# Block 0's taps split between two engines, and an order written out by hand that runs one block further

## The chip, the cores and the metric

The kernel runs on one core of a Trainium2 chip. The metric is device time in microseconds, the median of three runs: 1071.19 us before the change (1070.69 to 1071.75). The engines are named as in the profile: PE (TensorE, the matrix products), DVE (VectorE), ACT (ScalarE), POOL (GpSimd), and SP (SyncE), whose queue starts the transfers here.

## The reference

A causal attention of seven taps comes first. For every token and each of 8 heads a softmax over 7 numbers weights the token's own row and the 6 rows before it; a head is 24 of the 192 channels. Its output, 16384 tokens by 192 channels, goes through a feed-forward layer of 2048 columns with the gate `h * sigmoid(1.702 h)`:

```python
w = softmax(weight_gen, axis=-1)                      # (4, 4096, 8, 7)
x_unf = x_pad[:, idx, :].reshape(B, S, K, H, group)   # 7 rows for each token
x = np.einsum('bshk,bskhg->bshg', w, x_unf)           # (4, 4096, 192)
h = x.reshape(16384, 192) @ w_in                      # (16384, 2048)
g = h / (1 + exp(-1.702 * h))
out = g @ w_out                                       # (16384, 192)
```

The weights arrive as 64-bit floats and the output is 32-bit. The precision wanted is that of 32-bit products; most of the kernel reaches it with several 16-bit ones.

## The kernel before

**Tiling.** The 16384 tokens are cut into 32 blocks of 512, and the 2048 hidden columns into 16 slices of 128. One block times one slice is a unit, numbered 0 to 511. For a unit, PE fills one PSUM bank with h (128 columns by 512 tokens). In the program's order list `W.n` is the part of h that comes from channels 0 to 127 (line 446 to 449 from block 1 on, line 442 in block 0), and `X.n` does the part from channels 128 to 191 for the four units 4n to 4n+3 together. `gt` and `gm` are the gate (a tanh on ACT, line 469, and a product on DVE, line 474); `gh` and `gl` split the gated value into two 16-bit halves (ACT line 479, DVE line 481), after which the bank is free; `S.n` multiplies it by the output weights (line 495 to 497).

**Attention.** `a2.3` is step 3 of block 2: POOL multiplies 768 numbers in each partition by a tap's weights (line 190), and `a2.3p` adds them to the sum (line 206). The softmax steps are `s2.0` to `s2.6`: a maximum on DVE (line 154), a subtraction on POOL (line 156), an exponential on ACT, a sum and a reciprocal on DVE (lines 160 and 168), a product on POOL (line 174).

**Between the two.** `c2.0` finds block 2's largest value for its scale (DVE line 273, then one small PE product called `top`, line 255). `x2.0` to `x2.2` split the block into 16-bit parts (ACT line 312, DVE line 315), and `tu2` and `xd2` start the transposing transfers `xt` and a copy of part of it, `xd` (lines 321 and 325) on SP's queue.

**Block 0** is different: it is not split, and PE works on its 32-bit numbers. Its taps are multiplied one by one, five on DVE and two on POOL (`dtap`, `ptap`), two pairs are summed on DVE (`sum`), and PE turns and adds what is left (`tr.n`, line 231). `keep` copies the result to SBUF (lines 303 and 306). Meanwhile ACT and DVE narrow the weights: `nm`, `nb`, `n1`, `n2` from 64 to 32 bits (lines 374 to 394), and `na`, `bin`, `bout`, `ph`, `pl`, `ps` to 16-bit halves, of which `pl` is DVE's (line 421). `hold.A`, `hold.B` and `hold.C` let POOL copy 8 numbers out of a weight tile (line 615), so that POOL goes on only when DVE has finished that tile.

**What sets the order.** Every engine works through its own instructions in program order. Up to unit 31 (blocks 0 and 1) that order is the list ORDER, in which units take turns in four banks (`few = 2 * NF`, lines 433 to 435). From block 2 on a planner emits units by sixes in six banks, and each side step (scales, split, softmax, attention) has a due place in units. Since no place lies before `few`, the first planned block's scale is asked for right at that border (line 649).

## Time and profile before

| | |
|---|---|
| median of three runs | 1071.19 us |
| the profiled execution, as timed | 1072.55 us |
| its span, first to last instruction | 1070.3 us |
| busy in the span | PE 99%, DVE 80%, POOL 68%, ACT 64% |
| granted TensorE clock, mean | 0.995 |

PE is nearly always busy, so the time of this kernel is PE's work plus whatever PE waits for. All of what it waits for lies in the first 120 us: the slices of the page show PE busy to nine tenths or more from there to the last slice but one. The profiled execution is 2.25 us longer than its span and 1.36 us longer than the median.

### The profile page before, as it was taken

How to read it: one execution, taken by the hardware profiler on the slowest of the kernel's cores; microseconds unless marked ns; L12 is line 12 of the kernel's file. 1: busy time of each engine (PE TensorE's matmuls, PEld its weight loads, DVE VectorE, ACT ScalarE, POOL GpSimd, SP SyncE). 2: the span in 40 equal slices, each digit the busy share in tenths (PEclk: the TensorE clock that was granted, in tenths of full speed). 3: DMA queues.
4: the chain of work that ended last, by engine and by line, in shares of the span. 5: the costliest groups of instructions: out<-in, count | busy, mean ns of one | idle time of the engine just before them, and what ended most of it. 6: DMA issues, size and time to landing. Idle time of an engine off the chain costs nothing.

```text
span 1070.3 us, 22014 instructions
## 1 busy us (share of the span) xinstructions
...
## 2 busy tenths in 40 slices
...
GB/s 312 105 52 18 93 31 79 33 18 94 33 91 19 69 43 33 93 25 39 79 18 93 33 93 17 33 78 33 94 33 86 23 33 79 33 31 36 16 34 15
DMA packets 73454, 60.70 MB, mean 57 GB/s; under 512 B 60556, under 2 KB 66188, under 8 KB 71816
## 3 DMA queue, kind: packets, MB, share of 16 engines
...
q14 instruction: 34, 0.28, 0.1%
q10 hardware_dynamic: 288, 0.20, 0.1%
...
## 4 chain that ended last, share of the span: by engine, by line
PE 90%; DVE 4%; ACT 3%; POOL 2%; issue 1%; POOLq 0%; ACTq 0%
PE o L495 16%; PE o L497 15%; PE o L496 15%; PE h L446 10%; PE h L447 10%; PE h L449 10%; PE h L448 10%; PE h L463 5%; PE tr L231 1%; POOL acc L206 1%; POOL prod L190 1%; ACT g L479 1%; DVE g L474 1%; DVE h L474 0%; ACT wos L382 0%
## 5 line engine op out<-in xcount | busy, mean ns | idle before, releaser
L495 PE MATMUL o<-wos,g 128*128 128x192 f16 x1984 | 489.4, 247 | 0.0
L497 PE MATMUL o<-woh,g 128*128 128x192 f16 x1984 | 488.6, 246 | 0.0
L496 PE MATMUL o<-wol,g 128*128 128x192 f16 x1984 | 488.6, 246 | 0.0
L474 DVE SCALAR_TENSOR_TENSOR h<-th,h 128x512 f32<-128x512 f32 x496 | 335.9, 693 | 167.4 <-ACT th L469 159.3
L469 ACT ACTIVATE th<-h,s 128x512 f32<-128x512 f32 x496 | 332.5, 688 | 212.9 <-PE h L464 126.2
L206 POOL TENSOR_TENSOR acc<-acc,prod 128x768 f32<-128x768 f32 x186 | 344.6, 1852 | 14.4
L481 DVE SCALAR_TENSOR_TENSOR g<-g,h 128x512 f16<-128x512 f16 x496 | 338.3, 683 | 12.9 <-ACT g L479 1.2
L479 ACT ACTIVATE g<-h 128x512 f16<-128x512 f32 x496 | 296.5, 598 | 51.0 <-DVE h L474 51.0
L190 POOL TENSOR_TENSOR prod<-xb,wb 128x768 f32<-128x768 f32 x186 | 291.9, 1569 | 10.9
L495 PEld LDWEIGHTS <-g 128*128 128x128 f16 x1984 | 194.2, 98 | 73.8 <-issue 34.9
L496 PEld LDWEIGHTS <-g 128*128 128x128 f16 x1984 | 194.3, 98 | 35.6 <-issue 0.7
L497 PEld LDWEIGHTS <-g 128*128 128x128 f16 x1984 | 194.3, 98 | 0.0
L446 PE MATMUL h<-xt,w0l 128*128 128x512 f16 x496 | 188.7, 380 | 1.6 <-DVE s L261 1.3
L449 PE MATMUL h<-xt,wth 128*128 128x512 f16 x496 | 188.7, 381 | 0.0
L448 PE MATMUL h<-xt,w0h 128*128 128x512 f16 x496 | 188.7, 381 | 0.0
L447 PE MATMUL h<-xt,w0h 128*128 128x512 f16 x496 | 188.7, 381 | 0.0
L174 POOL TENSOR_TENSOR wb<-wb,wr 128x224 f32<-128x224 f32 x31 | 17.8, 575 | 209.0 <-DVE wr L168 198.0
L315 DVE SCALAR_TENSOR_TENSOR xs<-acc,s,xs 128x512 f16<-128x512 f32 (+1 forms) x62 | 91.7, 1518 | 0.3 <-ACT xs L312 0.3
L448 PEld LDWEIGHTS <-w0h 128*128 128x128 f16 x496 | 48.7, 98 | 59.0 <-issue 0.8
L449 PEld LDWEIGHTS <-wth 128*128 128x128 f16 x496 | 48.7, 98 | 59.0 <-issue 0.8
L463 PE MATMUL h<-xt,tl 64*128 64x512 f16 x248 | 67.9, 380 | 0.0
L464 PE MATMUL h<-xd,tl 64*128 64x512 f16 x248 | 67.9, 380 | 0.0
...
## 6 DMA issues: line engine op xcount, KB each, us to landing
...
```

The lines of the kernel that those rows point to most:

```text
L190: eng.tensor_tensor(to.rearrange("p j (h g) -> p (j h) g", g=G), xv, wv, ALU.mult)
L206: nc.gpsimd.tensor_tensor(acc, acc, t, ALU.add)
L446: nc.tensor.matmul(ps, lhsT=w0l[:, s], rhs=x0, start=start, stop=False)
L448: nc.tensor.matmul(ps, lhsT=w0h[:, s], rhs=x0, start=False, stop=False)
L449: nc.tensor.matmul(ps, lhsT=th_[:, s], rhs=x1, start=False, stop=stop)
L469: nc.scalar.activation(t, hp[u], AF.Tanh, scale=scale[u[0]][:, 4:5] if u[0] else SIG / 2)
L474: nc.vector.scalar_tensor_tensor(to, th.pop(u), 1.0, hp[u], ALU.add, ALU.mult)
L479: nc.scalar.activation(g[:, 0], hp[u], AF.Copy, scale=2.0**-12)
L481: nc.vector.scalar_tensor_tensor(g[:, 1], g[:, 0], -(2.0**12), hp.pop(u), ALU.mult, ALU.add)
L495: nc.tensor.matmul(o, lhsT=lo, rhs=wos[:, d], start=a and j % 2 == 0, stop=False, skip_group_check=True)
L496: nc.tensor.matmul(o, lhsT=hi, rhs=wol[:, d], start=False, stop=False, skip_group_check=True)
L497: nc.tensor.matmul(o, lhsT=hi, rhs=woh[:, d], start=False, stop=z, skip_group_check=True)
```

## The change

The attention of block 0 is divided by channels. DVE multiplies all seven taps for the first 6 heads (144 channels), and PE turns and adds channels 0 to 127 of them in one bank (`ta`, `tr`). POOL multiplies the last three heads (72 channels) and sums the taps in three groups for channels 128 to 191 (`tb`, with `p` for the sums); PE turns these three sums in another bank, two groups of 64 columns at a time (`trb`). `ka` and `kb` copy the results out in halves and quarters. Block 0's own softmax is subtracted on DVE instead of POOL.

ORDER now covers units 0 to 47, three blocks (`few = 3 * NF`), and the planner starts with block 3. The holds are no longer in the list. The first input weights are loaded ahead of the tail of channels.

On POOL, at the start of the program, this stood before (`tap` is block 0's, `acc` and `prod` are block 1's attention):

```order
L156 TENSOR_TENSOR wb<-wb,wm 128x224 x2
L184 TENSOR_TENSOR x_107<-wb,wr 128x224
L190 TENSOR_TENSOR tap<-xb,x_107 128x768 x2
L174 TENSOR_TENSOR wb<-wb,wr 128x224
L190 TENSOR_TENSOR acc<-xb,wb 128x768
```

and this stands there now:

```order
L193 TENSOR_TENSOR x_107<-wb,wr 128x224
L165 TENSOR_TENSOR wb<-wb,wm 128x224
L234 TENSOR_TENSOR rest<-xb,x_107 128x288 x2
L269 TENSOR_TENSOR rests<-rest 128x256
L234 TENSOR_TENSOR rest<-xb,x_107 128x288 x2
L269 TENSOR_TENSOR rests<-rest 128x256
L234 TENSOR_TENSOR rest<-xb,x_107 128x288 x2
L269 TENSOR_TENSOR rests<-rest 128x256
L234 TENSOR_TENSOR rest<-xb,x_107 128x288
L269 TENSOR_TENSOR rests<-rests,rest 128x256
L183 TENSOR_TENSOR wb<-wb,wr 128x224
L199 TENSOR_TENSOR acc<-xb,wb 128x768
```

Two long products became seven short ones and four sums, ahead of block 1's attention.

Further on POOL, in block 2's attention, where the first two holds stood:

```order
L206 TENSOR_TENSOR acc<-acc,prod 128x768
L156 TENSOR_TENSOR wb<-wb,wm 128x224
L615 COPY held<-w0l 128x8
L190 TENSOR_TENSOR prod<-xb,wb 128x768
L206 TENSOR_TENSOR acc<-acc,prod 128x768
L190 TENSOR_TENSOR prod<-xb,wb 128x768
L206 TENSOR_TENSOR acc<-acc,prod 128x768
L615 COPY held<-wol 128x8
```

and now, from block 2's second product on:

```order
L199 TENSOR_TENSOR prod<-xb,wb 128x768
L165 TENSOR_TENSOR wb<-wb,wm 128x224
L215 TENSOR_TENSOR acc<-acc,prod 128x768
L199 TENSOR_TENSOR prod<-xb,wb 128x768
L215 TENSOR_TENSOR acc<-acc,prod 128x768
L183 TENSOR_TENSOR wb<-wb,wr 128x224
L199 TENSOR_TENSOR prod<-xb,wb 128x768
L215 TENSOR_TENSOR acc<-acc,prod 128x768
```

No copy waits for a weight tile any more. The product with `wr` (line 183, step `s3.6` of block 3's softmax) now stands between block 2's third and fourth tap, and it needs a reciprocal from DVE. That reciprocal stands here on DVE, at the end of block 0 (`xs` is block 1's split, `w0l`, `tl` and `wol` are narrowed weights, `g` block 0's gates):

```order
L374 SCALAR_TENSOR_TENSOR xs<-acc,s,xs 128x4x128
L374 SCALAR_TENSOR_TENSOR xs<-acc,s,xs 128x4x64
L480 SCALAR_TENSOR_TENSOR w0l<-ri,sc,w0h 128x1024
L480 SCALAR_TENSOR_TENSOR tl<-rt,sc,th 128x1024
L533 SCALAR_TENSOR_TENSOR g_576<-th,h 128x512
L533 SCALAR_TENSOR_TENSOR g_583<-th,h 128x512
L480 SCALAR_TENSOR_TENSOR wol<-ro,sc,woh 128x1024 x2
L533 SCALAR_TENSOR_TENSOR g_605<-th,h 128x512
L480 SCALAR_TENSOR_TENSOR w0l<-ri,sc,w0h 128x1024
L177 RECIPROCAL wr<-wm 128x32
```

Before, the same stretch of DVE read:

```order
L315 SCALAR_TENSOR_TENSOR xs<-acc,s,xs 128x4x128
L315 SCALAR_TENSOR_TENSOR xs<-acc,s,xs 128x4x64
L260 TENSOR_REDUCE tm<-top 128x1
L261 TENSOR_SCALAR sums<-tm 128x1
L265 TENSOR_SCALAR sc<-sums 128x1
L266 TENSOR_SCALAR sc<-sc 128x1
L267 TENSOR_SCALAR sc<-sc 128x1
L283 TENSOR_SCALAR s<-s,sc 128x1
L474 SCALAR_TENSOR_TENSOR g_549<-th,h 128x512
L421 SCALAR_TENSOR_TENSOR tl<-rt,sc,th 128x1024
```

The scale for the input weights (`sc`) used to be worked out after block 1's split, and the output weights' scale and `wol` only in block 1; both scales now come ahead of the split, and two of the three `wol` pieces and both of `w0l` ahead of that reciprocal.

The diff, of the table its first and last lines only:

```diff
--- before.py
+++ after.py
@@ -20,27 +20,36 @@
 ONE = float(1 << 23)
 
 ORDER = """
-warm.11 s1.0 s0.0 s1.1 s0.1 s0.2 s0.3 s0.4 s0.5 s0.6 s0.7 ptap.1 dtap.5 dtap.2 tr.5 ptap.3 dtap.6 dtap.4
...
+s0.0 warm.8 s0.1 s0.2 s0.3 s0.4 s0.5 s1.0 s0.7 s0.6 s1.1 s1.2 ta.5 tb.0 tb.1 ta.6 tr.5 nm.i0 tb.1p ta.0 tr.6
...
+gt.47 a4.5p gm.47 gm.46 a4.6 gh.46 gh.47 gl.46 gl.47 a4.6p
 """
 TURNED = [a for a in ORDER.split() if a.startswith("tr.")]
+OTHERS = ((0, 1), (2, 3), (4, 5, 6))
 
 
 @with_exitstack
@@ -206,32 +215,72 @@
                 nc.gpsimd.tensor_tensor(acc, acc, t, ALU.add)
             yield
 
-    turned, taps, added = [], {}, []
-
-    def first_tap(k, by):
+    HA = -(-P // G)
+    turned, taps, added, rest = {}, {}, [], {}
+
+    def first_tap(k, eng):
+
         if k < K - 2:
-            t = apool.tile([P, J, D], F32, tag="tap", name="tap", bufs=K - 2)
+            taps[k] = apool.tile([P, J, HA * G], F32, tag="tap", name="tap", bufs=K - 2)
         else:
-            t = opool.tile([P, J, D], F32, tag="osb", name="tap")
-        taps[k] = t
-        tap(0, {"dve": nc.vector, "pool": nc.gpsimd}[by], t, k, near[by])
+            taps[k] = opool.tile([P, J, D], F32, tag="osb", name="tap")[:, :, 0 : HA * G]
+        near_tap(eng, taps[k], k, 0, HA)
+
+    def near_tap(eng, to, k, h0, h1):
+        n = h1 - h0
+        w = near["dve" if eng is V else "pool"].rearrange("p (j h) k -> p j h k", h=H)[:, :, h0:h1, k]
+        for j0 in range(0, J, 4):
+            xv = xb[0][:, j0 + k : j0 + k + J, h0 * G : h1 * G].rearrange("p j (h g) -> p j h g", g=G)
+            eng.tensor_tensor(
+                to.rearrange("p j (h g) -> p j h g", g=G), xv,
+                w.unsqueeze(3).to_broadcast([P, J, n, G]), ALU.mult,
+            )
 
     def add_taps(k, l):
-        nc.vector.tensor_tensor(taps[k], taps[k], taps[l], ALU.add)
+        nc.vector.tensor_tensor(taps[k][:, :, 0:P], taps[k][:, :, 0:P], taps[l][:, :, 0:P], ALU.add)
 
     def turn_tap(k):
 
 
-        if not turned:
-            turned.extend(ps_h.tile([P, N], F32, tag=f"h{i}", name="tr") for i in (1, 2))
+        if "a" not in turned:
+            turned["a"] = ps_h.tile([P, N], F32, tag="h1", name="tr")
         start, stop = not added, len(added) == len(TURNED) - 1
         added.append(k)
-        for ps, c, n in zip(turned, (0, P), (P, C1)):
-            for j in range(J):
-                nc.tensor.matmul(
-                    ps[:n, j * P : (j + 1) * P], lhsT=taps[k][:, j, c : c + n], rhs=ident,
-                    start=start and j == 0, stop=stop, skip_group_check=True,
-                )
+        for j in range(J):
+            nc.tensor.matmul(
+                turned["a"][:, j * P : (j + 1) * P], lhsT=taps[k][:, j, 0:P], rhs=ident,
+                start=start and j == 0, stop=stop, skip_group_check=True,
+            )
+
+    def rest_tap(k):
+
+        if not rest:
+            rest["sums"] = apool.tile([P, J, D], F32, tag="acc", name="rests").rearrange("p j d -> p (j d)")
+            rest["taps"] = apool.tile([P, J, D], F32, tag="prod", name="rest", bufs=1).rearrange("p j d -> p (j d)")
+        n = len(rest)
+        n = n % 2 * J * (D - (H - 3) * G)
+        t = rest[k] = rest["taps"][:, n : n + J * 3 * G].rearrange("p (j c) -> p j c", j=J)
+        near_tap(G_, t, k, H - 3, H)
+
+    def rest_sum(k):
+        g, at = next((g, i * J * C1) for i, g in enumerate(OTHERS) if k in g)
+        to = rest["sums"][:, at : at + J * C1].rearrange("p (j c) -> p j c", j=J)
+        a, b = (rest[l][:, :, 3 * G - C1 : 3 * G] for l in (g[0], k))
+        nc.gpsimd.tensor_tensor(to, a if k == g[1] else to, b, ALU.add)
+
+    def turn_rest(k):
+
+
+        if "b" not in turned:
+            turned["b"] = ps_h.tile([P, N], F32, tag="h2", name="tr")
+        i = [g[0] for g in OTHERS].index(k)
+        at, start, stop = i * J * C1, not rest.get("turned"), i == len(OTHERS) - 1
+        rest["turned"] = True
+        for q in range(J // 2):
+            nc.tensor.matmul(
+                turned["b"][:, q * P : (q + 1) * P], lhsT=rest["sums"][:, at + 2 * q * C1 : at + 2 * (q + 1) * C1], rhs=ident,
+                start=start and q == 0, stop=stop, skip_group_check=True,
+            )
 
     scale = {}
     inv_w, unit = sc[:, 0:1], sc[:, 1:2]
@@ -296,14 +345,24 @@
 
     x32 = [const.tile([P, N], F32, name=f"x32{c}") for c in range(2)]
 
-    def keep(n):
-
-
-        if n == 2:
-            nc.vector.tensor_copy(x32[1][C1:P], turned[1][0:C1])
+    def keep_a(n):
+
+        h = slice(n * N // 2, (n + 1) * N // 2)
+        if n:
+            nc.vector.tensor_copy(x32[0][:, h], turned["a"][:, h])
         else:
-            p = (P, C1)[n]
-            nc.scalar.copy(x32[n][0:p], turned[n][0:p])
+            nc.scalar.copy(x32[0][:, h], turned["a"][:, h])
+
+    def keep_b(n):
+
+
+        r, h = n % 2, n // 2
+        to = x32[1][h * C1 : (h + 1) * C1].rearrange("p (q r t) -> p q r t", r=2, t=P)[:, :, r]
+        of = turned["b"][r * C1 : (r + 1) * C1, 0 : N // 2].rearrange("p (q t) -> p q t", t=P)
+        if r == h:
+            nc.scalar.copy(to, of)
+        else:
+            nc.vector.tensor_copy(to, of)
 
     def split_x(blk):
         xs[blk] = t = tpool.tile([P, J, 2 * D], F16, tag="xs", name="xs", bufs=2)
@@ -517,7 +576,7 @@
 
 
     units = [(blk, f) for blk in range(NB) for f in range(NF)]
-    few = 2 * NF
+    few = 3 * NF
 
     def first(n):
 
@@ -551,8 +610,8 @@
     with tc.manual_schedule():
         load_w(0)
         load_x(0, 0, J)
+        load_in(0)
         load_tail(0)
-        load_in(0)
         load_in(1)
         load_x(0, J, XB * J)
         load_in(2)
@@ -578,15 +637,19 @@
             if a in ("s0.6", "s0.7"):
                 weights_near(("dve", "pool")[a == "s0.7"])
             elif k[0] == "s" and k[1:].isdigit():
-                step(k, softmax, int(k[1:]))
-            elif k in ("dtap", "ptap"):
-                first_tap(int(n), {"d": "dve", "p": "pool"}[k[0]])
+                step(k, softmax, int(k[1:]), G_ if int(k[1:]) else V)
+            elif k in ("ta", "pta"):
+                first_tap(int(n), V if k == "ta" else G_)
+            elif k == "tb":
+                (rest_sum if n[-1] == "p" else rest_tap)(int(n.rstrip("p")))
+            elif k == "trb":
+                turn_rest(int(n))
             elif k == "sum":
                 add_taps(*map(int, n.split(".")))
             elif k == "tr":
                 turn_tap(int(n))
-            elif k == "keep":
-                keep(int(n))
+            elif k in ("ka", "kb"):
+                (keep_a if k == "ka" else keep_b)(int(n))
             elif k == "warm":
                 warm(int(n), ident, P)
             elif k in ("nb", "nm", "n1", "n2", "na"):
@@ -613,21 +676,22 @@
                 step("tu" + k[2:], turn, int(k[2:]))
             elif k == "hold":
                 nc.gpsimd.tensor_copy(held, {"A": w0l[:, DFF - 8 :], "B": wol[:, 4 * QC - 8 : 4 * QC], "C": wol[:, 6 * QC - 8 :]}[n])
-            elif k == "lp2":
-                run(load_pair(2))
+            elif k[:2] == "lp":
+                run(load_pair(int(k[2:])))
             elif k == "W":
                 u = units[int(n)]
-                if u in hp:
-                    whole(u, False, True)
-                else:
+                new = u not in hp
+                if new:
                     bank(u)
-                    whole(u, True, False)
+                whole(u, new, not new)
             elif k == "X":
                 four = units[4 * int(n) : 4 * int(n) + 4]
-                for u in four[2:]:
-                    bank(u)
-                for u, v in zip(four[::2], four[1::2]):
-                    halves(u, v, u in four[:2], v in four[:2])
+                old = [u in hp for u in four]
+                for u, o in zip(four, old):
+                    if not o:
+                        bank(u)
+                for i in (0, 2):
+                    halves(four[i], four[i + 1], old[i], old[i + 1])
             elif k in ("gt", "gm"):
                 step("gate" + n, gate, units[int(n)])
             elif k in ("gh", "gl"):
@@ -637,14 +701,14 @@
                 for j in {"a": (0, 1), "b": (2, 3)}.get(n[-1], range(J)):
                     second(u, j)
             elif k == "st":
-                store(0, "ab".index(n))
+                store(int(n[:-1]), "ab".index(n[-1]))
             else:
                 raise ValueError(a)
 
         for a in ORDER.split():
             act(a)
 
-        for blk in range(3, NB):
+        for blk in range(4, NB):
             n = first(blk * NF)
             sc = [max(n - 12.2, few + 0.1), n - 7.9, n - 7.89, n - 7.3]
             plan(sc, scales(blk, lambda: "h0"))
@@ -652,11 +716,11 @@
             plan([n - 6.26], scales_out(blk))
             plan([n - 6.3, n - 6.2, n - 6.19], split_x(blk))
             plan([n - 6.15, n - 5], turn(blk))
-            if blk > 3:
-                if blk > 4:
+            if blk > 4:
+                if blk > 5:
                     plan([max(n - t, few + 0.01 - t / 1e4) for t in (48.2, 48.1, 42.1, 36.16, 36.15, 30.2, 30.1)], softmax(blk))
                 plan([n - 30 + 2.2 * ((k + 1) // 2) for k in range(2 * K - 1)], attend(blk))
-            if blk % XB == 0 and blk > 2 * XB:
+            if blk % XB == 0 and blk > 3 * XB:
                 plan([blk * NF - 56.5], load_pair(blk // XB))
 
         def seconds(six):
```

## Rows read from the trace of the kernel before

**Rows 1.** Waits of PE, whole span: us in total, times, longest.

```profile
PE top L255 <- DVE g L481: 3.5, 1, 3.5
PE h L446 <- DVE s L261: 1.3, 1, 1.3
PE h L442 <- DVE g L474: 1.2, 1, 1.2
PE top L255 <- DVE tf L250: 0.8, 1, 0.8
```

**Rows 2.** Stretches of 10 us, PE only: busy, granted clock (PEclk), DMA.

```profile
100.00:110.00 10.00, 5.87 (x39) 0.82 0.05 19
110.00:120.00 10.00, 9.27 (x55) 0.67 0.23 56
```

**Rows 3.** Timeline of PE at the border to the planner: start, duration, instruction.

```profile
107.48 0.19 PE L255 MATMUL top<-tf,ones 128*128 128x1 bf16 x1 [3.54 <-DVE g L481]
...
116.50 0.28 PE L495 MATMUL o<-wos,g 128*128 128x192 f16 x1
```

**Rows 4.** Timeline of DVE at the same place.

```profile
104.05 0.95 DVE L273 TENSOR_REDUCE top<-acc 128x1 f32<-128x768 f32 x1 [6.02 <-POOL acc L206]
```

**Rows 5.** Timeline of POOL: the second hold, then block 3's attention.

```profile
71.67 0.19 POOL L615 COPY held<-wol 128x8 f16<-128x8 f16 x1 [4.37 <-DVE wol L421]
...
79.75 1.54 POOL L190 TENSOR_TENSOR acc<-xb,wb 128x768 f32<-128x768 f32 x1
81.25 1.54 POOL L190 TENSOR_TENSOR prod<-xb,wb 128x768 f32<-128x768 f32 x1
...
84.76 1.54 POOL L190 TENSOR_TENSOR prod<-xb,wb 128x768 f32<-128x768 f32 x1
```

**Rows 6.** Timeline of PE at the start: block 0 turned, then unit 0.

```profile
8.41 10.60 PE L231 MATMUL tr<-ident,tap 128*128 128x128 f32 x80
18.94 1.99 PE L442 MATMUL h<-x,ri 128*128 128x512 f32 x4
```

**Rows 7.** Timeline of DVE at the start: four taps.

```profile
7.40 3.55 DVE L190 TENSOR_TENSOR tap<-xb,w 128x768 f32<-128x768 f32 x4
```

**Rows 8.** Page, costliest groups: after x the count, busy us, mean ns.

```profile
L474 DVE SCALAR_TENSOR_TENSOR h<-th,h 128x512 f32<-128x512 f32 x496 | 335.9, 693 | 167.4 <-ACT th L469 159.3
L174 POOL TENSOR_TENSOR wb<-wb,wr 128x224 f32<-128x224 f32 x31 | 17.8, 575 | 209.0 <-DVE wr L168 198.0
```

**Rows 9.** Store of one block, line 516: shortest/median/longest ns, first and last start.

```profile
L516 SPq DMA_DIRECT2D out_dram<-osb x31: 343/362/384, 71.0 to 1041.2; - x31
```

**Rows 10.** Timeline of DVE, block 1's split and a late scale.

```profile
52.39 1.15 DVE L315 SCALAR_TENSOR_TENSOR xs<-acc,s,xs 128x512 f16<-128x512 f32 x2 [0.28 <-ACT xs L312]
...
61.92 1.88 DVE L250 TENSOR_SCALAR tf<-groups,tm 128x4 bf16<-128x4 f32 x1
```

**Rows 11.** DVE's narrowing, tile wol, line 421: shortest/median/longest ns.

```profile
L421 DVE SCALAR_TENSOR_TENSOR wol<-ro,sc,woh x3: 1280/1286/1714, 69.1 to 74.6; 128x1024 f16<-128x1024 f32 x3
```

**Rows 12.** Timeline of POOL beside the longest of these (DVE, the last of the three).

```profile
73.45 1.82 POOL L206 TENSOR_TENSOR acc<-acc,prod 128x768 f32<-128x768 f32 x1
75.35 2.41 POOL L190 TENSOR_TENSOR prod<-xb,wb 128x768 f32<-128x768 f32 x1
```

**Rows 13.** Line 315 between 120 and 1040 us: busy us, mean ns.

```profile
L315 DVE SCALAR_TENSOR_TENSOR xs<-acc,s,xs 128x256 f16<-128x256 f32 x28 | 53.3, 1905 | 0.0
L315 DVE SCALAR_TENSOR_TENSOR xs<-acc,s,xs 128x512 f16<-128x512 f32 x28 | 35.5, 1268 | 0.0
```

**Rows 14.** SP's queue: block 2's transposing transfer, and the copy that waits for it.

```profile
90.82 1.46 SPq L321 DMA_TRANSPOSE xt<-xs  x1
94.53 0.61 SPq L325 DMA_DIRECT2D xd<-xt  x1
```

**Rows 15.** Timeline of PE: block 0's last `S` here (three of them), block 1's first matmul.

```profile
56.52 4.24 PE L492 MATMUL o<-ro,g 128*128 128x192 f32 x24
60.60 0.38 PE L446 MATMUL h<-xt,w0l 128*128 128x512 f16 x1
```

More of the change, by code (lines that the diff above doesn't have):

```diff
@@ L33 @@
-gt.15 xd1 s4.2 S.12 na.o4w pl.i2w gt.14 gm.15 W.16 hold.A a2.3 gm.14 W.17 bout.0 a2.3p X.4 s4.3 bout.1 W.18
-gt.17 bout.2 gt.16 W.19 a2.4 ph.o2w gm.16 S.13 gm.17 gh.16 co1 a2.4p gh.17 ps.o2w S.14a gl.17 S.14b gl.16
-ph.o0w S.15a S.15b pl.o0w ps.o0w W.20 st.a pl.o2w st.b S.16a gt.18 S.16b gt.19 S.17a hold.B gm.18 a2.5 S.17b
-gm.19 gh.18 W.21 gh.19 gl.18 a2.5p ph.o4w gl.19 S.18 ps.o4w X.5 pl.o4w W.22 gt.20 gt.21 a2.6 gm.20 W.23
-gm.21 gh.20 S.19 gh.21 gl.20 a2.6p gt.23 W.24 gt.22 gm.23 S.20 gl.21 gh.23 hold.C a3.0 gm.22 W.25 gl.23
@@ new lines @@
+nb.i0 tb.2 ta.4 tb.3 ta.3 trb.0 tb.3p s1.3 tr.4 nm.t0 ta.2 tb.4 nb.t0 n1.i0 tr.2 tb.5 ta.1 tb.5p tr.3
+sum.0.1 s1.4 tb.6 trb.2 s1.5 n2.i0 tr.0 tb.6p n1.t0 s1.6 trb.4 ka.0 ka.1 a1.0 nb.i1 W.0 kb.1 kb.2 nm.i1
+n2.t0 W.1 kb.0 a1.1 kb.3 n1.i1 nb.t1 X.0 nm.t1 a1.1p nb.i2w n1.t1 n2.i1 W.3 gt.1 n2.t1 gt.0 a1.2 gm.1 W.2
+gm.0 gt.3 W.5 gt.2 gm.3 a1.2p W.4 nm.o0 gm.2 X.1 nb.o0w a1.3 nm.o1 n1.o0 na.i0w W.7 n2.o0 a1.3p n1.o1 S.0b
+nm.i2 n2.o1 gt.4 S.0a gt.5 n1.i2 a1.4 S.1b nm.i3 gm.5 S.1a na.t0w n2.i2 W.6 a1.4p n1.i3 nm.o2 s2.0 S.2
@@ new lines @@
+nb.o2w s3.0 gm.4 a1.5 gt.6 W.9 n1.o2 gt.7 gm.6 S.3 n2.i3 s2.1 n2.o2 a1.5p nm.o3 W.8 s2.2 nm.o4 s2.3 S.4 gm.7
+nb.o4w a1.6 n1.o3 X.2 s2.4 n2.o3 na.i2w n1.o4 a1.6p n2.o4 S.5 gt.8 s2.5 bin.0 gt.9 s2.6 nm.o5 W.11 na.o2w
+a2.0 n1.o5 S.6 gm.8 n2.o5 a2.1 c1.0 W.10 na.o4w bin.1 S.7 na.o0w s3.1 bin.2 a2.1p c1.1 gt.10 W.12 c1.2
+ph.t0w bout.0 S.8 a2.2 gm.9 s3.2 pd.t0w gm.10 bout.1 gt.11 W.13 ph.i0w gm.11 a2.2p S.9 bout.2 x1.0 X.3 cg1
+s3.3 ph.o4w x1.2 x1.1 ph.o2w pl.i0w tu1 S.10 gt.12 pl.t0w gt.13 W.15 ps.o2w gm.12 S.11 s3.4 gm.13 gt.15
@@ new lines @@
+ph.o0w pl.o4w W.14 xd1 ph.i2w pl.o2w W.16 S.12 gt.14 gm.15 ps.o4w pl.i2w lp2 W.17 ps.o0w s3.5 S.13 gm.14
+s3.6 pl.o0w X.4 S.14a gt.16 co1 a2.3 gt.17 W.18 gm.16 gm.17 S.14b gt.18 a2.3p S.15a gh.16 gh.17 W.19 gl.16
+gm.18 a2.4 W.20 gt.19 gl.17 gh.18 S.15b gm.19 st.0a a2.4p W.21 gl.18 gh.19 st.0b s4.0 S.16a gl.19 S.16b a2.5
+S.17a X.5 S.17b gt.20 W.22 a2.5p gm.20 S.18 gt.22 gh.20 gm.22 W.23 a2.6 gt.21 gl.20 gh.22 S.19 gm.21 gt.23
+s5.0 W.24 gh.21 gm.23 s5.1 gl.21 a2.6p S.20 gh.23 gl.22 W.25 gl.23 c2.0 a3.0 S.21 X.6 s4.1 c2.1 S.22 gt.24
@@ new lines @@
+a3.1 gt.25 gm.24 W.26 gm.25 gh.24 W.27 c2.2 gt.26 a3.1p gl.24 gh.25 S.23 gt.27 gm.26 s5.2 W.28 gm.27 a3.2
+x2.0 gl.25 S.24 gh.26 gh.27 W.29 x2.1 s4.2 a3.2p gl.27 S.25 gl.26 X.7 S.26 x2.2 gt.29 a3.3 tu2 gt.28 W.30
+gm.28 S.27 gm.29 a3.3p gh.28 gh.29 gl.28 W.31 gt.30 gl.29 S.28 gt.31 a3.4 gm.30 s4.3 xd2 gh.30 W.32 s5.3 cg2
+s4.4 gm.31 a3.4p W.33 gl.30 gh.31 S.29 gl.31 co2 X.8 a3.5 S.30a gt.32 S.30b s5.4 gt.33 gm.32 W.35 a3.5p
+gm.33 gh.32 S.31a gl.32 gh.33 W.34 gt.35 gl.33 a3.6 W.36 gt.34 gm.35 st.1a S.31b gm.34 gh.35 S.32a a3.6p
```

18 lines of the change are left out of this document (5 added, 13 removed).

## Prediction

> **What bounds the kernel now.** I read the page first: PE is busy in nearly every slice, so the question is where PE waits or runs slowly. The list of PE's waits gives four places beside the first start: 3.5, 1.3, 1.2 and 0.8 us [rows 1], 6.8 us together (one of 0.2 us is left out). A table of windows then shows the granted clock: 0.82 of full speed in the stretch from 100 to 110 us and 0.67 in the next, 1.00 elsewhere [rows 2]. If the clock went from 2.4 to 1.2 GHz and back, half speed lasted 2 x 0.18 x 10 = 3.6 us of the first stretch and 2 x 0.33 x 10 = 6.6 us of the second, one piece of some 10 us around 106 to 117. PE stood still for 3.54 us just ahead of it, and its matmuls shorten again at 116.50 [rows 3]. From 107.5 to 116.5 it therefore worked at half speed, except for the 1.3 us in which it stood: 7.7 us of work, of which 3.8 us would not have been needed. So one event at the border between list and planner costs 3.5 + 1.3 + 3.8 = 8.6 us. Its cause is on DVE: the search for block 3's largest value sat 6.02 us until POOL had finished that block's attention at 104.0 [rows 4], and block 1's last gates, without which no bank comes free, were queued behind it. POOL was late because it had been made to wait, the longest hold alone 4.37 us [rows 5]. The other place is the start: PE turns block 0 in 80 records from 8.41 on, and unit 0 begins at 18.94 [rows 6].
>
> **The change, part by part.**
>
> *Start.* PE's 80 records in 10.60 us are 0.1325 us each [rows 6]. Now there are 6 turns of 4 matmuls and 3 of 2, 30 instead of 40, which at two records each are 60, or 7.95 us. The four taps on DVE took 3.55 us, 0.89 us for 768 columns [rows 7]; for 576, three quarters, that is 0.67 us, so the first is ready at about 8.1 instead of 8.4. PE done: 8.2 + 7.95 = 16.2; half a copy more (0.3 to 0.4 us) and unit 0 starts at about 16.5. Does another engine come later? DVE has seven taps, 4.7 us, one sum of at most 0.9, one piece of narrowing of 0.7 [rows 8] and small softmax steps of about 0.4: 7.4 + 6.7 = 14.1, when PE still has its last full turn ahead. POOL has eleven short instructions of 256 to 288 columns. The nearest row is 0.575 us for 224 columns [rows 8], and 1.54 us for 768 is the upper bound [rows 5]; by the straight line between them it is 0.69, by the bounds 6.3 to 17 us in all. From about 7.7 on (two steps of 0.57 behind a reciprocal that is there before DVE's first tap at 7.40) that ends at 15.3 (14 to 25); I take the line, and PE stays last. Gain 2.4 us, between 0 if POOL's products hardly shrink and 3.
>
> *The waits at 24 and 63 us.* The 1.2 us were a bank that DVE's gate had not freed, the 0.8 us a scale for the output weights. In the new order the first two gates stand ahead of the output weights' narrowing, and that scale is asked for before block 1 begins. I take both as gone, 2.0 us, and put what comes in their place into the allowance below.
>
> *Block 3's scale and the border.* POOL's new plan is a sum. One pair of product and addition takes 84.76 - 81.25 = 3.51 us, a block's first product 1.50 [rows 5], so a block takes 1.5 + 6 x 3.51 = 22.6 us, and each softmax step 0.57 [rows 8]. Block 0's rest ends at 15.3; one step, block 1 with one step in it, one more step, and block 2 as far as its third tap with one step: 15.3 + 0.6 + 22.6 + 0.6 + 0.6 + 1.5 + 7.0 + 0.6 = 48.8. Some small waits on DVE make it about 50. Then POOL needs the reciprocal that stands on DVE behind block 1's split, five narrowing pieces and three gates. The split began at 52.39 and took 1.15 us [rows 10]; moved by the earlier start it begins at 50.0. With 1.15, 5 x 1.28 [rows 11], 3 x 0.69 [rows 8] and 0.4, POOL goes on at 60.0. So without the holds POOL still waits some 10 us, in one place. From there: the step and block 2's other four taps with another step to 75.2, block 3 with one step to 98.3, a wait of up to 2 us for the next reciprocal, block 4 with two steps to 98.3 + 2 + 23.7 = 124.0; DVE's locks on POOL (below) add 1 to 2, so 125.5.
>
> DVE was ready for the 6.02 us wait at 98.0 [rows 4]. The same border now lies one block later. A block takes (1041.2 - 71.0) / 30 = 32.3 us from store to store [rows 9], 32.0 without the 8.6. So DVE gets there at 98.0 + 32.0 - 4.4 = 125.6, plus the allowance of 2 below: 127.6, about 2 us after POOL. Block 3's own scale is asked for inside block 2, near 101, with block 3 done at 98.3 to 99. Hence the 8.6 us go. The cover is thin: the narrowest place is block 2's scale, wanted near 75 to 76 with POOL done at 75.2.
>
> *DVE and POOL at the same time.* Without the holds some of DVE's work meets POOL's. A narrowing piece takes 1.28 us while POOL is held, and the one that met POOL took 1.71; POOL's product beside it took 2.41 instead of 1.54 [rows 11, 12, 5]. In the planned part the split's second piece, though half as long, takes 1.9 us where the first takes 1.27 [rows 13], while the two together took 1.15 with POOL idle [rows 10]: the second has to let one whole POOL instruction pass. "SBUF — State Buffer" of the Trainium skill, section "Who interferes with whom", says that a DVE instruction with two SBUF inputs and a GpSimd instruction that reads SBUF exclude each other for a whole instruction; the trace agrees by these rows. By that rule alone the removal of the holds speaks against the change, and what it would cost is the third rival.
>
> Here is how it works out: at the split and the five pieces POOL is waiting for its reciprocal, so they cost nothing extra; the last piece, and the two splits of blocks 2 and 3, meet it. Each of the two splits costs DVE 1.27 + 1.9 - 1.15 = 2.0 us, the last piece 0.4, and the two scale steps of the weights up to 1.4 each, since one took 1.88 us [rows 10] (0 if POOL is between instructions). All that is 4.4 us of lateness at least, up to 7.2, spread over five places. In the planned part PE bears it without a wait [rows 1]; how much it bears in four banks no row shows. Between nothing and 5 us I take 2.0 us of new waits, near the low end, because PE keeps second products to do while a gate is late.
>
> *Transfers.* Block 1's transposed input is needed when PE reaches unit 16. The copy behind the transpose started 3.71 us after it [rows 14], so from a split done at 51.2 to about 55. PE got to unit 16 at 60.60, with three second products in 4.24 us just ahead, 1.4 each [rows 15]. Now it has one fewer to do by then, so 60.6 - 18.9 - 1.2 - 1.4 = 39.1 us of work from unit 0 on, and it gets there at 16.5 + 39.1 = 55.6: just in time. If the split is 2 us late, so is PE.
>
> *Sum.* -2.4 - 2.0 - 8.6 + 2.0 = -11.0. The profiled execution was 1072.55 (span 1070.3 and 2.25 around it), so 1061.5; the median was 1.36 lower, so 1060.2.
>
> **The rivals.**
>
> *The early gains are lost again (1065).* PE starts earlier, but narrowing on ACT and DVE is then the bound in block 0, or four banks for a third block let DVE's locks through: 5 to 9 us of new waits instead of 2, so 1060.2 + 3 to 7. For it: block 1's input and unit 16 meet within half a microsecond. Against it: DVE was busy 80% of the span, and block 1 was run in four banks with hardly a wait [rows 1].
>
> *The event moves one block on (1069).* If POOL goes on 4 us later than 60.0, block 4 ends after DVE wants it; DVE waits, PE stops for 2 us or more and the clock halves again as in [rows 2]. That gives back most of the 8.6: 1060.2 + 8.6 = 1068.8. For it: the planner's rule at its border is the same, and the margin is 2 us. Against it: it bore 6.0 - 3.5 = 2.5 us of DVE's wait without a stop of PE.
>
> *Slower, by POOL met in the narrowing (1075).* If POOL is not yet at its reciprocal when the split begins, because its eleven short instructions take 1 us each rather than 0.69, it runs beside split and narrowing. Four DVE instructions stand there in a row, and each of the last three lets a whole POOL instruction of 1.5 to 1.8 us pass: some 6 us. Unit 16 takes its bank from a gate behind them, so PE stops for 5 us at the end of block 0 and loses 4 to the clock, as it did after 3.5 us of standing. POOL's own restart is 6 us late, block 2's scale with it, and block 4's at the border too: 4 + 4 again. That is 17 in place of the 2: 1060.2 + 15 = 1075. It decides itself at 3 to 4 us of lateness of POOL at 50 us.
>
> **How the numbers follow.** Forecast 0.62, gains lost 0.19, event moved on 0.11, slower 0.08. The forecast's own range is 1057.5 to 1063; for 8 times in 10 I go up to the second rival's 1068, and down to 1056.5, where the allowance costs nothing and the start gives 3. What a measurement can tell from no change is 0.2%, 2.1 us around 1071.2. Faster by more: the forecast, the lost gains and half of the event moved on, 0.62 + 0.19 + 0.055 = 0.86; within: 0.05; slower: 0.09.
>
> **What would show it.** In the profile after: unit 0's first matmul near 16.5 and 60 turning records ahead of it; a granted clock of 1.00 in every window from 100 to 130; DVE's search for block 4's value without a wait on POOL; one long wait of POOL near 50 to 60 us for a reciprocal; unit 16 near 55.6. The forecast is wrong if PE's list of waits shows more than 4 us outside the start, or if any stretch runs at the lower clock.

## The result, and the profile after

The changed kernel took 1061.88 us (median of 4 runs, 1061.33 to 1063.16), the kernel before 1071.2 us beside it (4 runs); the ratio is 0.9915 with a 95% interval of 0.9897 to 0.9932. The forecast was 1060.2. The profiled execution took 1063.16 us, with a span of 1061.4. In a later series the same kernel took 1061.88 us again (4 runs; ratio to the kernel before 0.9909, 0.9895 to 0.9923), and that profiled execution 1061.43, with a span of 1059.6.

PE's waits of the changed kernel over the whole span, which answer to [rows 1] (us in total, times, longest):

```profile
PE warm L604 <- DVE third L123: 4.0, 1, 4.0
PE h L501 <- DVE g L533: 1.7, 1, 1.7
PE h L505 <- DVE s L310: 1.0, 1, 1.0
PE tr L280 <- POOL rests L269: 1.0, 1, 1.0
PE h L505 <- DMA xt<-xs: 0.5, 1, 0.5
```

The first is the start, which the kernel before has too (4.05 us), and the fourth lies ahead of unit 0. What is left, 1.7 + 1.0 + 0.5 = 3.2 us, stands against 7.0 before (with the small one of 0.2). The last of them, for a transposed input, lies far behind the part that the change touches, as PE's timeline shows:

```profile
795.57 0.38 PE L505 MATMUL h<-xt,w0l 128*128 128x512 f16 x1 [0.51 <-DMA xt<-xs]
```

The stop of 3.5 us at the border is gone. So is the slower clock: the windows of PE that answer to [rows 2], busy time and granted clock, read

```profile
100.00:110.00 10.00, 10.00 (x84) 1.00 0.11 41
110.00:120.00 10.00, 10.00 (x93) 1.00 0.29 27
120.00:130.00 10.00, 10.00 (x84) 1.00 0.54 182
130.00:140.00 10.00, 8.97 (x72) 1.00 0.11 41
```

In the start [rows 6] PE no longer comes last. Its timeline has the end of the turning, unit 0 (16.74) and the 1.75 us wait in block 0:

```profile
16.19 0.71 PE L280 MATMUL tr<-ident,rests 128*128 128x128 f32 x4 [1.01 <-POOL rests L269]
16.74 1.89 PE L501 MATMUL h<-x,ri 128*128 128x512 f32 x4
...
24.44 1.99 PE L501 MATMUL h<-x,ri 128*128 128x512 f32 x4 [1.75 <-DVE g L533]
```

POOL's timeline shows why at the start (products of 0.67 us, line 234, and sums of 0.73 us, one of them 1.06, line 269), and then its one long wait and the end of block 4's attention:

```profile
12.08 1.34 POOL L234 TENSOR_TENSOR rest<-xb,x 128x288 f32<-128x288 f32 x2
13.50 1.06 POOL L269 TENSOR_TENSOR rests<-rest 128x256 f32<-128x256 f32 x1
14.64 0.69 POOL L234 TENSOR_TENSOR rest<-xb,x 128x288 f32<-128x288 f32 x1
15.41 0.73 POOL L269 TENSOR_TENSOR rests<-rests,rest 128x256 f32<-128x256 f32 x1
...
61.23 0.58 POOL L183 TENSOR_TENSOR wb<-wb,wr 128x224 f32<-128x224 f32 x1 [10.78 <-DVE wr L177]
...
76.72 1.81 POOL L215 TENSOR_TENSOR acc<-acc,prod 128x768 f32<-128x768 f32 x1
...
125.59 1.81 POOL L215 TENSOR_TENSOR acc<-acc,prod 128x768 f32<-128x768 f32 x1
```

DVE's timeline has the split of block 1 [rows 10] with narrowing pieces behind it, one piece of block 2's split, and the two searches for a block's largest value that the prediction named as narrow places. Neither has a wait, where block 3's had one of 6.02 us before [rows 4]:

```profile
51.91 1.14 DVE L374 SCALAR_TENSOR_TENSOR xs<-acc,s,xs 128x512 f16<-128x512 f32 x2
52.96 1.28 DVE L480 SCALAR_TENSOR_TENSOR w0l<-ri,sc,w0h 128x1024 f16<-128x1024 f32 x1
54.16 1.28 DVE L480 SCALAR_TENSOR_TENSOR tl<-rt,sc,th 128x1024 f16<-128x1024 f32 x1
...
56.55 2.48 DVE L480 SCALAR_TENSOR_TENSOR wol<-ro,sc,woh 128x1024 f16<-128x1024 f32 x2
...
78.56 0.95 DVE L322 TENSOR_REDUCE top<-acc 128x1 f32<-128x768 f32 x1
...
85.27 0.86 DVE L374 SCALAR_TENSOR_TENSOR xs<-acc,s,xs 128x512 f16<-128x512 f32 x1
...
128.72 0.94 DVE L322 TENSOR_REDUCE top<-acc 128x1 f32<-128x768 f32 x1
```

Last, PE's waits in the profiled execution of the later series, called the second execution below (the one above is the first):

```profile
PE h L505 <- DVE s L310: 1.0, 1, 1.0
...
PE tr L250 <- DVE tap L234: 0.5, 2, 0.3
PE h L501 <- DVE g L533: 0.3, 1, 0.3
PE o L551 <- DVE ro L453: 0.2, 1, 0.2
```

The waits of 1.7 and 0.5 us are not there, and its span is 1.8 us shorter; its wait of 0.3 us for a gate lies at 48.13 us, not at 24. ACT's timeline of the first execution names what was late at 24 us, a transfer of weights for which ACT waited 1.85 us:

```profile
20.58 0.77 ACT L433 ACTIVATE bits<-rt,third 128x512 int32<-128x512 uint32 x1 [1.85 <-DMA rt<-in_moe_w_in_dram]
...
23.06 1.09 ACT L528 ACTIVATE th<-h 128x512 f32<-128x512 f32 x2
```

The first gates (line 528) are queued behind that narrowing on ACT. In the second execution the same narrowing began at 18.75 and DVE's first gates at 21.88, against 23.71 here. This is 1.1 of the 1.8 us: the store of a block starts 1.07 us later in the first execution from block 0 (69.77 against 68.69) to the one at 775.42 us. The next store, at 807.62, is 1.74 us later: between them, at 795 us, one block's transposed input landed late (the copy that waits for it started 5.32 us behind the transposing transfer, against 4.10).

### The profile page after: what moved, and what is told of

It reads as the page before. It is cut to its first block, busy times and chain, and to the rows that moved or that the text cites. A ratio compares the mean times of both kernels' runs of the same rounds, so it can differ in the third digit from the quotient of the medians.

```text
span 1061.4 us, 21969 instructions
## 1 busy us (share of the span) xinstructions
PE 1049.1 (99%) x8733; PEld 738.6 (70%) x8733; DVE 854.6 (81%) x1525; ACT 688.4 (65%) x1210; POOL 731.2 (69%) x493
## 4 chain that ended last, share of the span: by engine, by line
PE 95%; DMA 2%; DVE 1%; ACT 1%; SPq 1%; issue 0%; ACTq 0%; DVEq 0%
PE o L554 16%; PE o L555 15%; PE o L556 15%; PE h L505 10%; PE h L508 10%; PE h L506 10%; PE h L507 10%; PE h L522 6%; PE o L551 2%; DMA rt<-in_moe_w_in_dram 1%; PE h L501 1%; PE h L516 1%; DMA xt<-xs 0%; DVE xs L374 0%; DVE h L533 0%
## 5 line engine op out<-in xcount | busy, mean ns | idle before, releaser
L374 DVE SCALAR_TENSOR_TENSOR xs<-acc,s,xs 128x512 f16<-128x512 f32 (+1 forms) x62 | 88.6, 1465 | 0.0
```

## The experiments

Times are set against the kernel before on the same chip; "after" means the changed kernel with 1061.88 us. The kernel before had medians of 1071.3 to 1072.0 us in the three series, so less than 1 us of difference from "after" says little.

### The border: was it the place of block 3's scale?

The kernel before, with the search for block 3's largest value asked for 3.1 units later:

```
-            sc = [max(n - 12.2, few + 0.1), n - 7.9, n - 7.89, n - 7.3]
+            sc = [n - 8.9 if blk == 3 else max(n - 12.2, few + 0.1), n - 7.9, n - 7.89, n - 7.3]
```

> The kernel before with its holds, but block 3's scale due three units later (35.1 instead of 32.1), so that DVE does three more gates before it waits for POOL. Theory: the loss at the border is one misplaced wait on DVE; POOL's lateness as such costs nothing. PE's stops of 3.5 and 1.3 us and the half clock go: 1062 to 1064, POOL's end of block 3 unchanged at 104. Rival: POOL's lateness binds somewhere else too (block 3's split or transfer comes late): 1067 or more, with a new wait of PE near 110 to 125 us.

1065.93 us (4 runs), ratio 0.995 (0.9936 to 0.9963): 5.4 us gained, the greater part of the 8.6, by moving one search. The stops and the half clock went as the text's theory said, but the time lies between its range and the rival's. Its list of PE's waits, without the start's, begins with

```profile
PE top L255 <- DVE tf L252: 1.7, 1, 1.7
PE tr L231 <- DVE tap L190: 1.2, 1, 1.2
PE h L442 <- DVE g L474: 1.2, 1, 1.2
```

The clock was 1.00 in every window. A wait of 1.7 us stays at the border, since now PE stands for the search itself. The wait at line 231 is of the start: in this execution a transfer came late.

### Was POOL late because of the holds?

The kernel before, with `hold.A`, `hold.B` and `hold.C` taken out of ORDER:

```
-... W.16 hold.A a2.3 ... S.17a hold.B gm.18 a2.5 ... gh.23 hold.C a3.0 ...
+... W.16 a2.3 ... S.17a gm.18 a2.5 ... gh.23 a3.0 ...
```

> The kernel before with its three holds taken out of the order, nothing else. Theory: the holds made POOL late, so block 3's scale was asked for too early by 6.0 us and 8.6 us were lost at the border. Without them POOL ends block 3's attention 3 to 6 us sooner (104.0 becomes 98 to 101; 6.8 us of holding gone, less what DVE's locks take from POOL), DVE's wait falls below 3 us, PE's stop and the low clock go, and DVE's lateness from POOL costs PE 1 to 3 us: 1064 to 1067. Rival: the locks cost as much as the holds, or POOL's waits for DVE's softmax steps take their place: 1070 to 1074, with the low clock still there.

1073.96 us (9 runs), ratio 1.0024 (1.0015 to 1.0034): slower, as the rival had it. The prediction's sentence that POOL was late because it had been held falls. POOL's timeline shows what came in the holds' place:

```profile
57.43 0.58 POOL L156 TENSOR_TENSOR wb<-wb,wm 128x224 f32<-128x224 f32 x1 [5.06 <-DVE wm L154]
57.97 2.57 POOL L190 TENSOR_TENSOR prod<-xb,wb 128x768 f32<-128x768 f32 x1
60.62 2.68 POOL L206 TENSOR_TENSOR acc<-acc,prod 128x768 f32<-128x768 f32 x1
...
93.48 0.57 POOL L174 TENSOR_TENSOR wb<-wb,wr 128x224 f32<-128x224 f32 x1 [6.75 <-DVE wr L168]
```

It ran on, met DVE's narrowing (2.57 and 2.68 us for what takes 1.54 and 1.82 [rows 5, 12]), and then waited 6.75 us for the reciprocal of a softmax step that stands late in DVE's own order. In the kernel before, with the holds, POOL's timeline already has a wait for that same step:

```profile
91.16 0.57 POOL L174 TENSOR_TENSOR wb<-wb,wr 128x224 f32<-128x224 f32 x1 [1.35 <-DVE wr L168]
```

So not the holds but DVE's reciprocal came last there, and from that step to the end of block 3's attention POOL takes 12.9 us with and without them. Without them DVE's search still waited for POOL:

```profile
106.38 0.95 DVE L273 TENSOR_REDUCE top<-acc 128x1 f32<-128x768 f32 x1 [5.97 <-POOL acc L206]
```

PE still stood for 3.5 us behind that, and its windows still have the slow clock:

```profile
110.00:120.00 10.00, 7.82 (x40) 0.66 0.10 40
```

Leaving out the holds alone does not get POOL done in time. What does in the change, by these rows, is the new place of the softmax steps together with the border one block later; no run takes the two apart.

### How much lateness does the new border bear?

The changed kernel, in which POOL repeats block 4's second product two or four times more, with the same values:

```
-                tap(blk, nc.gpsimd, t, k, w)
+                for _ in range(3 if blk == 4 and k == 1 else 1):    # 5 in the other
+                    tap(blk, nc.gpsimd, t, k, w)
```

> POOL repeats the second product of block 4 two times more (some 3.2 us of work, same values), behind its last wait for DVE, so that block 4's attention ends at about 130.6 us and not 127.4, while DVE asks for it at 128.7: DVE waits some 1.9 us. Theory A (the prediction's: PE bears some 2.5 us of such a wait in its banks before it stops): the clock stays 1.00, PE's wait near 135 us grows by at most 1 us, time 1062 to 1063. Theory B (no slack is left there, the 1.0 us wait of PE shows it): PE's wait grows by all of the 1.9 us, time 1063.5 to 1065.

> The same with four repeats, 6.5 us: block 4's attention ends at about 133.9 us, DVE waits some 5.2 us. Theory A (the prediction's second rival: the event of before comes again one block on, with a stop of PE of 2 us and more and half the clock for some 10 us behind it): a stage near 130 to 150 us at a granted clock of 0.65 to 0.85, time 1066 to 1070. Theory B (the stop costs its own length and the clock stays, as it stayed at 1.00 behind the 1.7 us wait): time 1064.5 to 1066, clock 1.00 everywhere.

With two: 1064.44 us (5 runs), ratio 0.9936 (0.9923 to 0.9948), 2.6 above after. In the profiled execution DVE's search waited 1.52 us for POOL, PE's wait near 135 us grew from 1.0 to 2.2, with 0.2 more for the search, and the clock stayed at 1.00. Its span is 2.7 us above the second execution's, and these waits are 1.3 of that; late transfers as in the first execution (waits of 0.84 us at 24 us and 0.58 at 796) are in it as well. The three slowest of the five have a mean clock of 0.998 instead of 0.999, so a short slow stretch is possible there; no trace shows one. With four: 1068.98 us (11 runs), ratio 0.9976 (0.9967 to 0.9984), 7.1 above after. DVE's search waited 4.74 us. Then the event of before is back, one block on, as the windows of PE with four repeats show:

```profile
130.00:140.00 10.00, 6.49 (x44) 0.83 0.00 0
140.00:150.00 10.00, 8.79 (x50) 0.66 0.22 64
150.00:160.00 10.00, 10.00 (x89) 1.00 0.12 24
```

and its timeline of PE, with the stop ahead of the slow stretch:

```profile
137.96 0.19 PE L305 MATMUL top<-tf,ones 128*128 128x1 bf16 x1 [3.39 <-DVE g L541]
...
141.21 0.58 PE L506 MATMUL h<-xt,w0l 128*128 128x512 f16 x1 [1.33 <-DVE s L311]
```

The first matmul behind it takes 0.58 us where it takes 0.38 at full clock. The prediction's second rival was this, at 1069. Here theory A of the second text held. With two repeats PE bore next to nothing of DVE's wait of 1.5 us: theory B of the first text held there.

### POOL met in the narrowing

The changed kernel, in which `s3.6`, for whose reciprocal POOL waits from 50 to 61 us, stands only behind block 2's attention:

```
-s3.6 pl.o0w X.4 S.14a ...          ... gl.23 c2.0 a3.0 S.21 ...
+pl.o0w X.4 S.14a ...               ... gl.23 c2.0 s3.6 a3.0 S.21 ...
```

> The changed kernel with one softmax step of POOL (block 3's product with its reciprocal) moved from between block 2's third and fourth tap to behind block 2's attention, so that POOL no longer waits 10.8 us for DVE at 50 to 61 us and works through block 1's split and the narrowing. Theory (the third rival of the prediction): DVE's row of split, split, w0l, tl lets POOL instructions pass; block 1's transposed input comes 3 to 5 us later, PE stops about as long before unit 16 and the clock may drop: 1066 to 1074. Against it: POOL being 10 us earlier costs nothing and the locks are short: within 1.5 us of 1061.9.

1068.74 us (7 runs), ratio 0.9976 (0.9965 to 0.9987), 6.9 above after. DVE's timeline of this kernel:

```profile
50.89 2.71 DVE L374 SCALAR_TENSOR_TENSOR xs<-acc,s,xs 128x512 f16<-128x512 f32 x2
53.53 2.56 DVE L480 SCALAR_TENSOR_TENSOR w0l<-ri,sc,w0h 128x1024 f16<-128x1024 f32 x1
56.01 2.83 DVE L480 SCALAR_TENSOR_TENSOR tl<-rt,sc,th 128x1024 f16<-128x1024 f32 x1
...
59.95 4.13 DVE L480 SCALAR_TENSOR_TENSOR wol<-ro,sc,woh 128x1024 f16<-128x1024 f32 x2
```

Split and four pieces took 12.23 us instead of 1.14 + 1.28 + 1.28 + 2.48 = 6.18, and POOL's products and additions beside them, from 55 us on, 2.4 to 2.7 us. PE waited 2.2 and 1.4 us for gates behind them, and its windows have a slower clock:

```profile
50.00:60.00 10.00, 7.76 (x35) 0.97 0.31 59
60.00:70.00 10.00, 8.57 (x40) 0.86 0.40 153
```

PE's timeline has the first stop and a matmul of 0.58 us behind it, as at half clock:

```profile
59.49 0.58 PE L505 MATMUL h<-xt,w0l 128*128 128x512 f16 x1 [2.24 <-DVE g L533]
```

The third rival's mechanism is real, and POOL's long wait is what keeps it off. Its price was 6.9 us rather than 15: block 4's scale was not late as well (its search, at 133.52 us, has no wait).

### The start: who is last, and is the gain carried through?

Eight matmuls more that warm PE, and sixteen:

```
-s0.0 warm.8 s0.1 ...
+s0.0 warm.16 s0.1 ...      # warm.24 in the other
```

> Eight further matmuls warm PE ahead of block 0, 2 to 3 us of work, so that unit 0 starts at about 18 to 19.5 us, nearly where the kernel before had it, with everything else of the change kept. Theory A (the start's gain is worth less than the 2.2 us it shows, since the narrowing binds the first 30 us and PE only waits for it at 24 us): PE's wait of 1.7 us goes, time 1061.9 to 1063. Theory B (the start's gain is carried through to the end): time 1064 to 1065.5, the waits of 1.7 and 0.5 us stay.

> Sixteen further matmuls warm PE ahead of block 0. The first eight of the run before cost 2.2 us of PE and moved unit 0 by only 0.46 us, because POOL's rest had been the last there; with eight more PE is the last by far and unit 0 starts at some 19.2 us, as in the kernel before (18.94). Theory A (the early start is carried through): unit 16 about 2 us later than the 57.0 to 58.1 seen, no wait for its input, time 1063.7 to 1064.8, so the start is worth its 2.2 us. Theory B (the first block's narrowing is the bound and PE only gets there earlier to wait): unit 16 within 0.7 us of 58, time 1061.5 to 1062.5.

With eight more PE began to turn at 9.86 instead of 7.62 us, and unit 0 moved by 0.45 us only. PE's timeline with eight more:

```profile
9.86 1.95 PE L250 MATMUL tr<-ident,tap 128*128 128x128 f32 x16
...
17.19 1.99 PE L501 MATMUL h<-x,ri 128*128 128x512 f32 x4 [0.29 <-DVE x L352]
```

1062.24 us (4 runs), ratio 0.9914 (0.99 to 0.9927), not to be told from after: since unit 0 did not move as expected, this run decides only that PE had some 1.8 us to spare. With sixteen more unit 0 began at 19.27 us, and PE's timeline shows unit 16 39.25 us behind it:

```profile
19.27 1.99 PE L501 MATMUL h<-x,ri 128*128 128x512 f32 x4 [0.48 <-DVE x L352]
...
58.52 0.38 PE L505 MATMUL h<-xt,w0l 128*128 128x512 f16 x1
```

1063.83 us (5 runs), ratio 0.9928 (0.9914 to 0.9941), 1.95 above after, and the fastest of the five (1063.45) is slower than every execution of the changed kernel. So the early start does reach the end, but not whole: the time is theory A's, and unit 16 (58.52 us) lies within 0.7 us of 58, as theory B had it. Of the 2.5 us by which unit 0 began later, unit 16 shows 1.5 against the second execution (57.03) and 0.4 against the first (58.10), where the late transfer had taken most of the early start away again. Its span of 1062.0, 2.4 longer than the second execution's, has a wait of 0.73 us at 508 us in it that the other lacks.

### The wait at 24 us

The first gates of units 0 to 3 ahead of the tail's narrowing (`nb.t1`, `nm.t1`, `n1.t1`, `n2.t1`, and `nb.i2w` with them, go behind `W.4`), and, in another kernel, the output weights' narrowing ahead of the second half of the input weights:

```
-kb.3 n1.i1 nb.t1 X.0 nm.t1 a1.1p nb.i2w n1.t1 n2.i1 W.3 gt.1 n2.t1 gt.0 ... W.4 nm.o0 gm.2 ...
+kb.3 n1.i1 X.0 a1.1p n2.i1 W.3 gt.1 gt.0 ... W.4 nb.t1 nm.t1 gm.2 n1.t1 nb.i2w n2.t1 nm.o0 ...

-kb.3 n1.i1 nb.t1 X.0 nm.t1 a1.1p nb.i2w n1.t1 n2.i1 ... n1.o0 na.i0w W.7 ... nm.i2 n2.o1 gt.4 S.0a gt.5 ...
+kb.3 n1.i1 X.0 a1.1p n2.i1 ... n1.o0 gt.4 W.7 ... nm.i2 n2.o1 gt.5 nb.i2w S.0a gm.5 n1.i2 a1.4 S.1b nb.t1 ...
```

> The changed kernel with the narrowing of the second tail of input weights moved on ACT and DVE behind the first four gates. Theory: the 1.75 us that PE stands at 22.7 us come from ACT, which waits 1.85 us for that tail's transfer (landed at 20.6) with the first gates queued behind it. The wait goes, 1.3 to 1.8 us less than the changed kernel: about 1060.3. Rival: the weights' transfers or ACT's own load bind the start anyway, so that the wait turns up at the next units or at the first output product: 1061.5 to 1062.5.

> In block 0 the four first gates of units 4 and 5 (gt.4, gt.5, gm.5) and the narrowing of the output weights' first half now stand ahead of the narrowing of the input weights' second half and of the tail. Theory A (PE's waits of the first 30 us are a queue on ACT and DVE that is simply full: narrowing plus first gates are the bound there, so that a reorder only moves the wait): PE's wait of 1.7 us at 24 us goes or shrinks, one of 1 to 2 us comes within the next 20 us, time within 1.5 us of 1061.9. Theory B (the wait is one late transfer met by one gate, which a better order avoids): no wait over 0.5 us before unit 16, time 1060 to 1060.8.

1063.27 us (5 runs), ratio 0.9924 (0.9912 to 0.9936), and 1063.64 us (5 runs), ratio 0.9923 (0.9909 to 0.9937): no gain. In the first the wait at 24 us was gone and one of 1.5 us for the output weights' narrowing (line 453) stood at 28.9 us, at the first output product as its rival had said. In the second there were two of 0.5 us, at 27.9 and 39.9 us, which fits neither of its theories. So two other orders moved the wait and gained nothing. That ACT and DVE have no room to spare in these 30 us is a likely reading and not shown: in the second execution the unchanged order had a wait of only 0.2 us there.

### What is left of the border

The changed kernel with block 4's search 3 units later:

```
-            sc = [max(n - 12.2, few + 0.1), n - 7.9, n - 7.89, n - 7.3]
+            sc = [n - 8.9 if blk == 4 else max(n - 12.2, few + 0.1), n - 7.9, n - 7.89, n - 7.3]
```

> Only block 4's search for its largest value is put 3 units later in the planner (51.1 instead of 48.1 units into the block), so it is asked for at some 134 us, not 128.7. Theory A (the wait of 1.0 us near 135 us is what is left of the border's event: gates queued behind that step): it goes, time 1060.5 to 1061.3. Theory B (the step found POOL already done by 1.3 us, so nothing is queued behind it, and the wait comes from the burst of second products just ahead): time 1061.6 to 1062.4, the wait stays within 0.3 us.

1063.08 us (5 runs), ratio 0.9924 (0.9911 to 0.9936). The wait of 1.0 us went down to 0.2, as theory A had it, but PE stood 1.65 us for the search itself, the same wait as in the first experiment. No gain. The changed kernel as it is was run beside these:

> The changed kernel itself on the same chip as the three variants, so that they can be set against it directly: 1061.3 to 1063.2 as before.

Its numbers stand with the result. No variant was faster by more than these measurements can tell.

## Why the prediction was right, and where it was not

| term | predicted | first execution | second execution |
|---|---|---|---|
| start | -2.4 | -2.2 | -2.2 |
| waits at 24 and 63 us (and the one of 0.2) | -2.0 | -2.2 | -2.2 |
| border, with the clock | -8.6 | -8.6 | -8.6 |
| new waits | +2.0 | +3.2 | +1.5 |
| sum | -11.0 | -9.8 | -11.5 |
| span, measured | | -8.9 | -10.7 |

The forecast span of 1059.3 lies 2.1 below the first execution and 0.3 below the second. The term that was mis-sized is the new waits, 2.0 against 3.2, in the execution in which two transfers landed late. That the second comes so near is partly luck: 0.5 us less of new waits stand against 0.8 us of work that the sum does not have (below).

*The step to the median.* In medians the change brought 9.3 us where the sum has 11.0. The 8.6 us of the border are its price in the profiled execution, whose mean clock was 0.995. Of 41 other executions of the kernel before two had 0.995, at 1072.18 and 1072.49 us; the other 39 had 0.997, with a median of 1071.32. An estimate from these rounded means: half the clock lasted some 2 x 0.003 x 1070 = 6.4 us in most of them instead of some 10, and cost some 2 us less. The prediction took the whole 8.6 off the slower execution and then took off the 1.36 us by which it lay above the median, so it most likely counted a part twice. Without that step it would have said 1061.5.

*Start.* The size was right (16.74 for 16.5) and the order of arrival wrong: "PE stays last" failed. POOL's products took 0.67 us and its sums 0.73, about the line's 0.69, but one sum took 1.06 beside a sum of DVE's, and some 0.08 us lay between its instructions, so the rest ended at 16.14, not 15.3. PE's side was ready with some 1.8 us to spare.

*Waits at 24 and 63 us.* The second is gone. The first was taken as gone and came back as 1.75 us in one execution and not in the other, with another cause: not the output weights' narrowing, but the tail's, whose data came late.

*POOL's plan.* The sum gave 48.8 to 50 us up to the reciprocal and POOL got there at 50.45 (61.23 - 10.78). The split began at 51.9 rather than 50.0 (at 50.8 in the second execution), and POOL went on at 61.23 rather than 60.0 (at 60.15 in the second). Block 2 was done at 78.53 rather than 75.2, since a product took 2.53 us beside a narrowing piece and POOL waited 1.35 us for a maximum. At the narrowest place it still came in time, because DVE, too, was there only at 78.56. The 0.03 us between them are more than chance: the maximum for which POOL waited (line 163) stands on DVE only four gate instructions ahead of that search, and in the second execution and in the run with POOL met in the narrowing the two came 0.03 and 0.04 us apart again. Block 4 was done at 127.40 and wanted at 128.72: predicted were 125.5 and 127.6. The margin was 1.3 us instead of 2, and the profiled run with two repeats shows that past it each microsecond costs PE about one.

*Border.* Right in mechanism, and in price for the profiled execution: its 8.6 us are gone, the clock is 1.00 throughout, and the runs with the search moved and with POOL made late take the event away and bring it back. What failed is the sentence on POOL's lateness (the holds), in whose place the runs show DVE's late reciprocal. The argument against the second rival failed as well, that PE bears 2.5 us of such a wait: in this place it bore 0.2 of DVE's 1.5 us, and with four repeats 1.0 of 4.7. The rival did not come about because POOL was early enough.

*DVE and POOL at the same time.* The splits of blocks 2 and 3 were priced at 2.0 us of lateness each. DVE's pieces took 0.86 and 0.74, then 0.75 and 0.48 us, against 1.15 for the whole [rows 10]: 0.45 and 0.1 us more. POOL paid instead, with additions of 2.14 us at 85.66 and 2.35 at 110.41 where 1.82 is usual [rows 12]; the second started 0.07 us behind DVE's piece. In [rows 13] DVE had been the one to pay. "SBUF — State Buffer" of the Trainium skill, section "Who interferes with whom", has a sentence for this that the prediction did not weigh: "Issue order, not op shape, decides who blocks." The traces agree on both sides, with 1.9 us for a split's half in [rows 13] and 2.35 for POOL here.

*Transfers.* Unit 16 was forecast at 55.6 and began at 58.10 and 57.03. Of the 2.5 us in the first execution 1.75 are the wait at 24 us and 0.2 the later unit 0; the rest is work, 58.10 - 16.74 - 1.75 = 39.6 us from unit 0 to unit 16 where 39.1 were predicted. "Just in time" with the transposed input was too tight: PE did not wait for it, and the copy that waits for it started at 56.94, 1.2 us ahead of unit 16 (55.85, again 1.2, in the second execution).

*What stays open.* Sum and span differ by 0.9 and 0.8 us in the same direction: from unit 0 on PE has that much more to do than before, waits and clock taken off (1061.4 - 16.74 - 3.2 = 1041.5, against 1070.3 - 18.94 - 7.0 - 3.8 = 1040.6). Some of it, 0.5 us, lies ahead of unit 16 (39.6 against 39.1; 0.7 in the second execution). Block 2 runs in four banks now and has four `X` groups instead of 2 2/3, which may be the rest; that was not tried. Why the weights' transfer and the transposing one land later in some executions was not settled either.
